# Retention and an ELU block on one core: the order of the first loads, VectorE's order, and eight products of a blank tile

## The chip, the core and the metric

The kernel runs on one core of a Trainium2 chip. TensorE (PE in the profile; its weight loads are PEld), VectorE (DVE), ScalarE (ACT) and GpSimd (POOL) each work through their own list of instructions in order, and SyncE (SP) issues nearly all DMAs in order. The metric is the device time of one execution in microseconds; lower is better. Five runs of the kernel before are shown.

## The reference

```python
def _attn_ref(q, k, v):                       # B, H, S, D = 4, 8, 768, 64
    gamma = 1.0 - 2.0 ** (-5.0 - np.arange(H))
    for t in range(S):
        state = gamma * state + einsum('bhd,bhe->bhde', k[:, :, t], v[:, :, t])
        y[:, :, t] = D ** -0.5 * einsum('bhd,bhde->bhe', q[:, :, t], state)
def _moe_ref(x, w_in, w_out):                 # x: 3072 x 512, w_in: 512 x 2048, w_out: 2048 x 512
    h = x @ w_in
    return np.where(h > 0, h, np.exp(np.minimum(h, 0)) - 1) @ w_out
```

The output of the retention, `y`, turned to (tokens, heads times D), is the `x` of the second block. All is in single precision; the weights reach the kernel as 64-bit floats, and the kernel itself turns their bits into 32-bit ones ("decodes" them).

## The kernel before

The 3072 tokens are worked on in six blocks (`tb`) of 512, and a block in four chunks of 128 tokens. A chunk `m` has two tiles, each 512 KB: `qk` (turned q and k) and `kvn` (plain k and v), fetched by `load(m)`. The weights come in 16 pieces of 1024 KB; `load_piece` fetches one into one of three buffers `wraw`. A piece goes through `prepare` on ScalarE (two activations for each part, L142 and L144; two parts where it is called with 2) and `decode` on VectorE (four operations for each part, L165, L168, L171, L174). `decode(True)` is a generator that stops after each of these, and `take(n)` goes on by n of them. After its last step `decode` calls `load_piece` for the next piece.

Retention of a pair of chunks: `score_products` (64x64 products into `sc`), `mask_pair` on VectorE (scores times `cmask`, written over k), `scale_v` (v times `vf`; on VectorE for chunk 0, on ScalarE for chunk 3, else on GpSimd), `state_products` (64x64 products into `kv`), `state_sum` (a copy on ScalarE for the first state, L317, else a sum on VectorE, L319), and `outputs`, a generator: products of scores and v (L341), products of q and the states (L367) with two tiny `seen` copies on VectorE between their halves (L355), and last the product with the table `etab` (L376) that makes `xb`, the input of the second block. In PSUM, `sc`, `kv` and `y` take buffers of the pool `ps_r` (four); four more banks are named a (two), b and d (`bank`).

`plain_first` then multiplies `xb` by the first weights, four products to a tile: `pa` twice, `pb`, `pd`, `hp`, for the first half of the tokens. Scores, states and outputs of chunks 2 and 3 stand between these. After that the second half of the tokens and all later weights follow, and from the second block on Strassen's scheme of seven products.

The order is written out by hand: the schedule is manual, and each engine does its instructions in the order in which the program issues them. The opening is: loads (piece 0, chunks 0 and 1, piece 1, chunks 2 and 3, piece 2), tables (`pos_t`, `lny`, `post`, `etab`, `vf`, `cmask`), then the first pair of chunks with the decoding of piece 0 between its steps, then `plain_first`. The stage buffers make a fourth piece wait until piece 0 is decoded.

## Time and profile before

| | us |
|---|---|
| median of 5 runs | 646.27 (645.45 to 649.8) |
| the profiled execution | 645.79 |
| its span in the profile | 643.7 |
| TensorE busy | 629.4 |
| VectorE busy | 494.8 |
| ScalarE busy | 240.6 |
| GpSimd busy | 39.7 |

The profile is of one execution. Its span goes from the first to the last instruction; the execution's own time is 2.1 us longer. Times in the views count from the start of the span. Busy shares are means over the whole span; the change touches only the first 35 us or so.

### The profile page before, as it was taken

The numbers are of one execution on the slowest core, as the hardware profiler recorded it, in microseconds if no ns is written. First come the engines' busy times: TensorE is split into PE (matmuls) and PEld (weight loads), VectorE is DVE, ScalarE is ACT, GpSimd is POOL, SyncE is SP. The second block draws the span as 40 slices with busy tenths as digits, with TensorE's granted clock in tenths as the row PEclk, the third lists the DMA queues.
The fourth block names the chain that finished last, engine by engine and source line by source line (L and its number), as shares of the span: only waits on it lengthen the run. The fifth ranks groups of instructions, "written<-read, shape, count | busy, mean of one in ns | idle before, by whom it ended". The sixth has DMA issues, their size and how long they took to land.

```text
span 643.7 us, 15861 instructions
## 1 busy us (share of the span) xinstructions
PE 629.4 (98%) x6512; PEld 542.6 (84%) x6512; DVE 494.8 (77%) x887; ACT 240.6 (37%) x463; POOL 39.7 (6%) x38
## 2 busy tenths in 40 slices
PE   4999999999999999999999999999999999999998
PEld 3774444548889999989999989999988999988997
DVE  5789789998979776589767488867568959557976
ACT  6467641204542112546111465211464311356311
POOL 1001100000360000110000110000020000000000
PEclk9999999999999999999999999999999999999999
DMA  8638978999388789802789810789940688710694
GB/s 340 251 131 314 328 237 245 291 275 285 118 270 270 236 261 321 275 11 62 248 284 307 286 78 24 220 278 279 300 163 3 198 264 277 221 43 1 217 306 165
DMA packets 85208, 139.71 MB, mean 217 GB/s; under 512 B 6672, under 2 KB 38800, under 8 KB 82832
## 3 DMA queue, kind: packets, MB, share of 16 engines
q1 hardware_dynamic: 85136, 138.70, 66.4%
q8 instruction: 51, 0.84, 0.5%
q14 instruction: 21, 0.17, 0.1%
HBM read 114.56 MB, written 24.12 MB: 215 GB/s over the span
## 4 chain that ended last, share of the span: by engine, by line
PE 81%; DVE 9%; DMA 3%; SPq 2%; issue 2%; POOL 2%; ACT 1%; POOLq 0%; DVEq 0%
PE pa L811 20%; PE pa L772 10%; PE pd L811 9%; PE hp L454 6%; PE pb L811 5%; PE pa L726 4%; PE pb L772 4%; PE qa L772 3%; PE pd L726 2%; PE qd L772 2%; PE pd L772 2%; PE y L341 2%; SPq L505 2%; PE y L367 2%; PE kv L307 2%; PE sc L276 2%
## 5 line engine op out<-in xcount | busy, mean ns | idle before, releaser
L819 ACT COPY ms<-pa 128x128 f32<-128x128 f32 x104 | 27.6, 266 | 145.5 <-PE pa L811 143.9
L811 PE MATMUL pa<-ts,wq 128*128 128x128 f32 x560 | 74.1, 275 | 0.3 <-ACT ms L819 0.3
L811 PE MATMUL pd<-ts,wq 128*128 128x128 f32 x552 | 73.2, 275 | 0.0
L811 PEld LDWEIGHTS pa<-ts,wq 128*128 128x128 f32 x560 | 68.5, 192 | 0.8 <-ACT ms L819 0.5
L811 PEld LDWEIGHTS pd<-ts,wq 128*128 128x128 f32 x552 | 67.1, 192 | 0.3 <-DVE res L823 0.2
L811 PE MATMUL pa<-gC,wq 128*128 128x128 f32 x480 | 64.7, 278 | 0.0
L422 ACT ACTIVATE r<-r 128x512 f32<-128x512 f32 x96 | 60.5, 630 | 3.0
L811 PEld LDWEIGHTS pa<-gC,wq 128*128 128x128 f32 x480 | 59.0, 192 | 1.3
L421 ACT ACTIVATE r<-gC 128x512 f32<-128x512 f32 x64 | 39.9, 624 | 32.3 <-DVE gC L780 32.3
L823 DVE TENSOR_TENSOR res<-pd,ms 128x128 f32<-128x128 f32 x68 | 19.4, 286 | 36.9 <-PE pd L811 35.6
L250 POOL TENSOR_TENSOR kvn<-kvn,vf 128x512 f32<-128x512 f32 x22 | 25.8, 1177 | 345.8 <-DMA kvn<-in_qkv_dram 182.6
L425 DVE SCALAR_TENSOR_TENSOR gC<-r,gC 128x512 f32<-128x512 f32 x64 | 41.8, 685 | 0.7 <-ACT r L422 0.7
L688 DVE TENSOR_TENSOR ts<-gC,ts 128x512 f32<-128x512 f32 x60 | 41.2, 687 | 1.0
L688 DVE TENSOR_TENSOR ts<-gC 128x512 f32<-128x512 f32 x60 | 40.9, 682 | 0.0
L811 PE MATMUL pb<-gC,wq 128*128 128x128 f32 x240 | 32.8, 277 | 0.1
L468 PE MATMUL pa<-gC,w_s 128*128 128x512 f32 x64 | 30.6, 600 | 0.0
L811 PEld LDWEIGHTS pb<-gC,wq 128*128 128x128 f32 x240 | 29.5, 192 | 0.8 <-DVE gC L425 0.8
L844 ACT COPY res<-pa 128x128 f32<-128x128 f32 x34 | 9.0, 266 | 56.2 <-PE pa L811 53.2
L780 DVE TENSOR_TENSOR gC<-qa,gC 128x512 f32<-128x512 f32 x8 | 5.5, 692 | 25.1 <-PE qa L772 18.3
L552 ACT COPY m<-pa 128x512 f32<-128x512 f32 x24 | 13.9, 580 | 25.6 <-PE pa L772 14.2
L772 PE MATMUL pa<-xt,w_b 128*128 128x256 f32 x96 | 23.0, 382 | 0.0
L772 PE MATMUL pa<-xt,w_s 128*128 128x256 f32 x96 | 23.0, 382 | 0.0
(206 smaller groups left out, 1229.1 us busy)
## 6 DMA issues: line engine op xcount, KB each, us to landing
wq<-scratch_dram SPq DMA_DIRECT2D x277, 256.0 KB, 4.4
wraw<-in_w_dram SPq DMA_DIRECT2D x16, 1024.0 KB, 5.8
qk<-in_qkv_dram SPq DMA_DIRECT2D x24, 512.0 KB, 6.9
kvn<-in_qkv_dram SPq DMA_DIRECT2D x24, 512.0 KB, 7.4
scratch_dram<-w_s SPq DMA_DIRECT2D x8, 512.0 KB, 7.2
scratch_dram<-so SPq DMA_DIRECT2D x8, 512.0 KB, 5.5
out_dram<-res SPq DMA_DIRECT2D x14, 256.0 KB, 4.2
scratch_dram<-gT SPq DMA_DIRECT2D x12, 256.0 KB, 3.8
```

Of the source, the lines that this page charges most:

```text
L250: eng.tensor_tensor(out=kv[:, 1], in0=kv[:, 1], in1=vf[:, i].unsqueeze(2).to_broadcast([C, H, D]), op=ALU.mult)
L421: nc.scalar.activation(e, h, AF.Relu, scale=-1.0)
L422: nc.scalar.activation(e, e, AF.Exp, scale=-1.0)
L425: nc.vector.scalar_tensor_tensor(g, e, -1.0, h, ALU.add, ALU.max)
L454: nc.tensor.matmul(hp, lhsT=w[n][:, fi, j // 2, j % 2, :], rhs=xb[:, j, :], start=(j == 0), stop=(j == 3))
L468: nc.tensor.matmul(ops[d], lhsT=wo[:, row, (d if row else d ^ 2) * P :][:, 0:P], rhs=g_plain[row * NF + f], start=(n == 0 and row == 0), s ...
L688: sub = lambda o, x, y: nc.vector.tensor_tensor(out=o, in0=x, in1=y, op=ALU.subtract)
L726: nc.tensor.matmul(ps[:, f, :], lhsT=lhs[f], rhs=xs[j][k], start=(begin and f == 0), stop=True, skip_group_check=True,)
L772: nc.tensor.matmul(ps[:, fi, :], lhsT=w[:, fi, j2, :], rhs=x[:, j2, :], start=(j in (1, 7) and fi == 0 and j2 == 0), stop=(j2 == 1), skip_ ...
L811: nc.tensor.matmul(ps, lhsT=w[:, f, :], rhs=ts[j][k][:, f, :], start=(begin and f == 0), stop=(f == 3), skip_group_check=True,)
L819: nc.scalar.copy(m, ps)
L823: nc.vector.tensor_tensor(out=o, in0=x, in1=y, op=ALU.add)
```

## The change

It touches the opening alone.

- The order of loads becomes chunk 0, piece 0, chunk 1, piece 1, chunks 2 and 3, piece 2. A held load waits for another's landing: `hold` has GpSimd copy one element of the landed tile into the tile that is to be loaded, and the load waits for that copy. `qk` and `kvn` of chunk 1 are held behind those of chunk 0, piece 1 behind piece 0, chunks 2 and 3 behind `kvn` of chunk 1, and piece 2 behind piece 1.
- The tables' small operations come first, `post` and `etab` last. GpSimd makes `pos_s` ahead of `pos_t`.
- A tile `blank` is set to 0 by VectorE before all else. `unread` multiplies it by itself into a buffer of bank a that nobody reads: two products of 512 columns ahead of the first scores, and six of 256 columns: one behind these scores, one behind the first outputs, two behind the second scores, and two ahead of `plain_first`.
- The first `outputs` write to banks b and d instead of the pool `ps_r`.
- VectorE's order: none of piece 0 is decoded ahead of the first scores; the first mask comes ahead of the scaling of chunk 0. `scale_v` of chunk 1 moves from GpSimd to VectorE and stands behind the second mask. The eight steps of piece 0 then stand thus: two behind the first states' sum, two behind the first state of chunk 1, two behind the `seen` copies, two behind `xb`.
- On TensorE the first outputs come ahead of the second scores.

```diff
-    def load(m):
+    def load(m, behind=(None, None)):
...
+        hold(qk_, behind[0])
+        nc.sync.dma_start(qk_, qkv[m, :, 0:1024])
...
+        hold(kv_, behind[1])
+        nc.sync.dma_start(kv_, qkv[m, :, 1024:2048])
         raw[m] = (qk, kv)
+
+    def hold(t, other):
+
+        if other is not None:
+            nc.gpsimd.tensor_copy(t[0:1, 0:1], other[0:1, 0:1])
...
-    def load_piece():
+    def load_piece(behind=None):
...
+            hold(t[:, :, 0].bitcast(FP32), behind)
             nc.sync.dma_start(t.rearrange("p c w -> p (c w)"), w_bits[n].bitcast(U32))
...
-    load_piece()
-    load(0)
-    load(1)
-    load_piece()
-    load(2)
-    load(3)
-    load_piece()
...
+    blank = hpool.tile([P, TB], FP32, name="blank", tag="h")
+    nc.vector.memset(blank, 0.0)
...
+    load(0)
+    load_piece()
+    load(1, [raw[0][x][:, 0, 0] for x in range(2)])
+    load_piece(staged[0][:, :, 0].bitcast(FP32))
+    late = raw[1][1][:, 0, 0]
+    load(2, (late, late))
+    load(3, (late, late))
+    load_piece(staged[1][:, :, 0].bitcast(FP32))
...
-        eng = nc.vector if m == 0 else nc.gpsimd
+        eng = nc.vector if m < 2 else nc.gpsimd
...
-        y = [ps_r.tile([P, 2 * 2, 2, D], FP32, name="y", tag="r") for _ in range(2)]
+        if first:
+
+            y = [bank(x).rearrange("p a (b x d) -> p (a b) x d", b=2, x=2) for x in "bd"]
+        else:
+            y = [ps_r.tile([P, 2 * 2, 2, D], FP32, name="y", tag="r") for _ in range(2)]
...
+    warm = bank("a").rearrange("p a b -> p (a b)")
+
+    def unread(count, n):
+        for _ in range(count):
+            nc.tensor.matmul(warm[:, 0:n], lhsT=blank[:, 0:P], rhs=blank[:, 0:n], start=True, stop=True, skip_group_check=True)
+
     prepare(2)
     piece = decode(True)
-    take(4)
+    unread(2, TB)
     sc = [ps_r.tile([P, 2, HP, D], FP32, name="sc", tag="r") for _ in range(2)]
     score_products(sc, 0, 0, 0)
+    mask_pair(sc, 0)
     scale_v(0)
-    scale_v(1)
-    mask_pair(sc, 0)
+    unread(1, TH)
     kvs = [ps_r.tile([P, 2, HP, D], FP32, name="kv", tag="r") for _ in range(2)]
     state_products(kvs, 0, 0, 0, range(2))
-    score_products(sc, 0, 0, 1)
     state_sum(kvs, 0, 0, 0, 0)
     state_sum(kvs, 0, 0, 0, 1)
-    mask_pair(sc, 1)
-    take(2)
-    prepare()
     y = outputs(0, 0, True)
     next(y)
+    unread(1, TH)
+    score_products(sc, 0, 0, 1)
+    take(2)
+    mask_pair(sc, 1)
+    scale_v(1)
+    unread(2, TH)
     state_products(kvs, 0, 0, 1, [0])
     next(y)
     state_sum(kvs, 0, 0, 1, 0)
-    take()
+    prepare()
+    take(2)
 
     next(y)
+    take(2)
     next(y)
     state_products(kvs, 0, 0, 1, [1])
+    unread(2, TH)
+    next(y, None)
     take(2)
-    next(y, None)
     state_sum(kvs, 0, 0, 1, 1)
     scale_v(2)
     decode_all()
```

## Prediction

> **What bounds the kernel now.** I read the page first, then the chain of work that ended last over the first 50 us, then the timeline and the DMA issues of that stretch.

> ```profile
> PE 629.4 (98%) x6512; PEld 542.6 (84%) x6512; DVE 494.8 (77%) x887; ACT 240.6 (37%) x463; POOL 39.7 (6%) x38
> PE   4999999999999999999999999999999999999998
> ```

> TensorE is busy for 629.4 of 643.7 us, and its idle time lies in the first slice of 16 us and in the tail. A change confined to the opening can win only what TensorE loses there. The chain (start, us, what) shows two losses.

> ```profile
> 2.23 3.41 ACT etab L209 x4
> ...
> 18.29 0.69 DVE xb L376
> 18.99 0.04 issue
> 19.03 5.40 PE pa L443 x16
> 24.43 1.09 PE sc L276 x64
> 25.52 0.93 PE kv L307 x64
> ...
> 30.11 1.09 PE y L341 x64
> 31.20 0.48 PE y L367 x32
> 31.68 0.02 issue
> 31.70 0.25 DVE seen L355 x2
> ...
> 34.62 3.45 PE pa L443 x16
> ```

> The first big products wait for `xb` until 19.03. And the same sixteen products of `pa` take 5.40 there and 3.45 at 34.62: a loss of 1.95 us to a slow array clock. (The view of busy time by stretch gives a granted clock of 1.00 for both, so here the durations decide.) The chain to 19.03 runs through ScalarE and VectorE, not through TensorE. What loads allow is in the issues; first the queue's timeline (start, us), then the view of DMA issues over each single issue, whose last number is us to landing.

> ```profile
> 0.74 0.38 SPq L121 DMA_DIRECT2D wraw<-in_w_dram  x1
> 1.64 0.42 SPq L104 DMA_DIRECT2D kvn<-in_qkv_dram  x1
> 2.88 0.45 SPq L104 DMA_DIRECT2D kvn<-in_qkv_dram  x1
> 3.38 0.49 SPq L121 DMA_DIRECT2D wraw<-in_w_dram  x1
> ```

> ```profile
> wraw<-in_w_dram SPq DMA_DIRECT2D x1, 1024.0 KB, 4.9
> kvn<-in_qkv_dram SPq DMA_DIRECT2D x1, 512.0 KB, 7.1
> kvn<-in_qkv_dram SPq DMA_DIRECT2D x1, 512.0 KB, 8.4
> wraw<-in_w_dram SPq DMA_DIRECT2D x1, 1024.0 KB, 10.4
> ```

> So piece 0 lands at 5.6, the pair of chunk 0 at 8.7, that of chunk 1 at 11.3, piece 1 at 13.8: strictly in turn, 2.5 us for 1024 KB and 1.3 for 512 KB.

> **Loads.** In the new order `qk`, `kvn` of chunk 0 and piece 0 are issued at once. The first landing took 4.9 us, 2.5 of them transfer, so 2.4 are start. Chunk 0 then lands at 0.74+2.4+1.3 = 4.4 and 5.7, piece 0 at 8.2; by the row in which the same 2 MB had landed, at 8.7. I take 8.5: chunk 0 comes 3 us sooner, piece 0 2.9 us later. The eight holds are one-element copies on GpSimd; the nearest rows are its 128x1 memset (0.10) and its 48-element iota (0.21). With 0.4 for the issue a held load starts about 0.7 after the landing that it waits for, and 0.9 later data flows (first issue 0.74, DMA busy from about 1.6). `qk` of chunk 1 is thus ready at 6.0, while piece 0 streams to 8.2; piece 1 at 10.1, while chunk 1 streams to about 10.9; chunk 2 at 12.6, while piece 1 streams to about 13.4. The cover is 0.8 us at the tightest, so I cost the holds at nothing. Behind each hold on SyncE stand all later loads, and the consumers with least room are the eight ScalarE scalings of chunk 3 (landing 20.3 before, done 22.4, wanted near 24.1): 1.7 us of room, so a gap below that costs nothing, a longer one 1:1.

> **VectorE and ScalarE up to `xb`.** The blank memset is bounded by the 64x1 memset (0.06) and a 128x512 pass (0.43); I take 0.43. With the small operations now first, `post` ends near 4.2 and the four `etab` activations (3.41) near 7.6. That is below 8.5, so this reordering costs nothing; it is also the floor for piece 0's preparation. The new path hangs on piece 0, because ScalarE runs in order: the copy of the first state (L317) stands behind piece 0's four preparations, and on VectorE the next sum stands behind that copy, with all the rest behind it. From 8.5: four preparations 2.66 (5.68 to 8.34) → 11.2; copy 0.37 → 11.6; sum 0.42 → 12.05; two decode steps 0.9 → 12.95; two masks 0.76 → 13.7; scaling chunk 1, moved from GpSimd (1.04) to VectorE (0.68) → 14.35; eight state products, half of the row of 1.14 at the slow clock and a quarter at the fast one, with their latency 0.4 → 14.75; sum 0.42 → 15.2; two decode steps 1.4 → 16.55; two `seen` copies 0.35 → 16.9; two decode steps 0.9 → 17.8; two `xb` products 1.29 → 19.1. The first `pa` starts at 19.15, 0.1 later than before. What the earlier chunk 0 and the shorter front give is eaten by the late piece. The first outputs in banks b and d spare two slots of the r pool; no wait there shows, since `y` waited for the mask at 12.51: nothing.

> **The blank products.** At the fast clock one product of 512 columns costs 0.86 (16 records of 512 columns, 6.87 us), at the slow one twice that. The first two fill about 1.3 to 4.7; `qk` lands at 4.4, so scores lose 0.3 to work that VectorE holds up anyway. The middle ones lie in waits for VectorE. The last two end near 17.3+0.3+0.86 = 18.5, 0.6 before `xb`: free while the clock is up. In exchange `pa` takes 3.45.

> Whether they lift the clock, and whether it stays, no row shows; the bounds are all of 1.95 us or nothing of it. The row next to it is a stretch without any 128x128 product (busy us of TensorE in it):

> ```profile
> 12.50:16.20 3.70, 3.64 (x104) 1.00 1.01 405
> ```

> TensorE was busy for 3.64 of 3.70 us and yet `pa` ran slow after it: the 64x64 products do not lift the clock, while dense ones did within 3.5 us (from 19.03; by 22.6 a product takes its later 0.22 us). The two opening blank products are 3.4 us of the dense kind, so I take it that they lift it. [...] Between the pair after the second scores (ends near 11.0) and the state products at 14.35 TensorE has nothing for 3.3 us. This is the weak place. I take it as held, since dense products stand in every 4 us or so.

> **After `pa`.** `pa` ends at 19.15+3.45 = 22.6, against 24.43: 1.83 gained. But VectorE now carries two decode steps behind `xb` that it had done before, and loses the 2.42 us in which it waited for scores. From 19.1: these two 1.38, sum 0.33, piece 1 3.94 → 24.75; masks 1.2, sums 1.83, half of piece 2 2.34, `seen` 0.25 → 30.35. TensorE: scores and states 2.02 → 24.6; `pb` waits for piece 1 to 24.8; `pb`, `pd` 3.65, outputs 1.57 → 30.0; it then waits for `seen` to 30.4. Before, that point was 32.0. The gain is 1.6 us: 0.2 of the clock's gain goes at `pb`, and the outputs wait 0.4 where they had waited 0.3. From there the same work follows, and the later pieces have 4 us and more of room.

> The profiled execution took 645.79 (span 643.7 and 2.1 around it), 0.48 below the median of 646.27. The sum: 645.79-1.6 = **644.2**.

> **Rivals.**
> 1. The clock falls back in the gap. Then the last small products (0.65+0.57) and the two blank ones (1.7) run slow from 16.9 and end at 19.8, now in front of `pa`. The dense run starts at 18.1. If the clock rises 3.4 us later, `pa` ends at 24.2 (0.25 gained); if after twice that, at 25.9 (1.4 lost). Time 645.5 to 647.2, say 646.4, above before. [...] For it: 3.3 us almost without work. Against: a dense pair just ahead.
> 2. The held loads do not queue behind piece 0 but share the engines with it. Piece 0 then lands with chunk 1, near 11.3, 2.8 late; the gap grows past 6 us, the clock is lost, `pa` starts at 21.95 and takes 5.40. Time 648.7; it is worse than before as soon as piece 0 lands later than 10.1. Against: landings strictly in turn in all rows.
> 3. Piece 0 lands before `etab` ends (7.6), or a link of my chain is shorter. At the floor the path starts at 7.65 and wins 0.85 more: 643.35. Two overlapped links, masks and scaling for instance (1.4), would give 642.0. For it: the chain is serial by my estimate only.
> 4. The change gains nothing because blank data does not count as activity: as rival 1, 645.5 to 647.2; counted with it.

> **Numbers.** Forecast 0.55, own range 643.4 to 645.2; rivals 1 and 4 together 0.26; rival 2 0.05; rival 3 0.14, about two thirds of it below 643. Range 642.9 to 646.7: it leaves out about 0.1 below (the far part of rival 3) and 0.1 above (the upper end of rival 1, and rival 2). A measurement of this kernel tells about 0.5%, 3.2 us, from no change; that is 642.6 and 649.0. Faster than that: most of rival 3's far part and a little of an unseen link, 0.11. Slower: rival 2 with a longer gap in the loads, 0.06. Same: 0.83.

> **What would show it.** Right: piece 0 landing near 8.5; copy of the state on ScalarE near 11.2; `pa` from about 19.15 in 3.45; the second half of the next pair's outputs at 30.4 after a wait for `seen`. Wrong: `pa` x16 above 4 us (clock lost), a wait of the scores or of `pb` for a DMA (loads held too long), or `pa` starting below 18.3 (the path isn't the one I followed).

## The result and the profile after

The changed kernel takes 649.26 us (median of 27 runs, 647.9 to 654.1), the kernel before 646.9 beside it: a ratio of 1.0044, with a 95% interval of 1.0032 to 1.0057. By the ratio that is 2.8 us slower (the medians are 2.4 apart), less than the 0.5% that I set as the bound, but far from the 1.6 us gain of the forecast and outside the range. The profiled execution took 650.8 (span 648.9, 1.9 around it), 5.0 above that of before, and 1.5 above its own median. All sums below are made between these two traces, and the sizes are then corrected by the runs.

The page of after, TensorE's busy row and the granted clock by slice:

```profile
PE 635.9 (98%) x6528; PEld 545.0 (84%) x6528; DVE 496.4 (76%) x889; ACT 240.8 (37%) x463; POOL 39.7 (6%) x45
PEclk9899999998999999999999999999999999999999
```

There are 16 more products and two slices with an 8: TensorE is as busy as before in share, but 6.5 us longer (629.4 before), part of it at the lower clock. The timeline of TensorE in the opening (start, us, engine, line, product, tile, count, then idle time before it):

```profile
1.45 3.74 PE L977 MATMUL pa<-blank 128*128 128x512 f32 x4 [1.45 <-DVE blank L197]
5.12 0.69 PE L290 MATMUL sc<-qk 64*64 64x64 f32 x32
11.28 1.13 PE L977 MATMUL pa<-blank 128*128 128x256 f32 x4
14.39 0.62 PE L321 MATMUL kv<-kvn 64*64 64x64 f32 x14 [1.98 <-DVE kvn L264]
18.82 2.07 PE L977 MATMUL pa<-blank 128*128 128x256 f32 x4
20.68 4.31 PE L461 MATMUL pa<-xb,w_a 128*128 128x256 f32 x16
32.64 0.57 PE L385 MATMUL y<-qk,kvn 64*64 64x64 f32 x23 [0.27 <-DVE seen L373]
```

The blank products did lift the clock: the first scores take 0.69 where they had taken 1.13, and four blank records take 1.13. But four of the same records take 2.07 at 18.82, in front of `pa`, which starts at 20.68 and not at 19.15. The second half of the next outputs, forecast at 30.4, comes at 32.64, against 32.00 before. The view of busy time by stretch shows why, and shows the same thing again 130 us later (stretch, its length, busy us of PE, PEld, DVE, ACT, POOL, then the granted clock, DMA share, GB/s):

```profile
5.00:15.20 10.20, 5.80 (x177) 4.28 (x179) 3.89 (x10) 5.40 (x10) 1.43 (x8) 1.00 0.98 363
15.30:22.00 6.70, 6.06 (x88) 5.13 (x79) 6.14 (x13) 2.11 (x2) 1.09 (x2) 0.50 1.00 358
148.40:151.80 3.40, 1.36 (x7) 0.90 (x6) 3.37 (x7) 0.00 (x0) 0.00 (x0) 1.00 1.02 285
151.80:155.20 3.40, 3.40 (x9) 2.70 (x8) 3.30 (x6) 1.83 (x3) 0.00 (x0) 0.50 1.03 333
155.20:160.00 4.80, 4.80 (x24) 4.20 (x23) 1.94 (x4) 0.81 (x3) 0.00 (x0) 1.00 0.93 271
```

Setting the starts of the same products in the two traces against each other, product by product, gives where the 5.2 us of span went: +0.64 at the end of the opening; nothing up to 147 us; +3.4 between 148 and 155; +1.2 at 222; nothing from there to the end.

**At 149 us.** The waits of VectorE around 125 us and of TensorE around 149 (who waits, for what: us in total, times, longest), before and after:

```profile
DVE m L509 <- DMA scratch_dram<-m: 0.8, 1, 0.8
PE pa L602 <- DVE xt L395: 0.3, 1, 0.3
```

```profile
DVE m L527 <- DMA scratch_dram<-m: 2.2, 1, 2.2
PE pa L620 <- DVE xt L413: 2.0, 1, 2.0
```

VectorE stands 1.4 us longer for a store of `m`, has hardly any slack behind it (before, it is busy for 20.25 of the 21 us from 127 to 148), and 20 us later TensorE waits 2.0 us for `xt`; behind that wait the clock is at 0.50 from 151.8 to 155.2 (the fourth row above), which costs 1.6 more. What the store waits for is in the timeline of SyncE, before and after:

```profile
98.27 0.35 SPq L121 DMA_DIRECT2D wraw<-in_w_dram  x1
111.34 0.44 SPq L121 DMA_DIRECT2D wraw<-in_w_dram  x1
120.55 3.87 SPq L505 DMA_DIRECT2D scratch_dram<-m  x4
```

```profile
109.77 0.98 SPq L131 DMA_DIRECT2D wraw<-in_w_dram  x1
112.55 5.55 SPq L131 DMA_DIRECT2D wraw<-in_w_dram  x1
121.01 5.61 SPq L523 DMA_DIRECT2D scratch_dram<-m  x4
```

Before, piece 14 of the weights was issued at 98.27 and piece 15 at 111.34. After, piece 14 goes out at 109.77 and piece 15, with two stores between them, at 112.55; the two megabytes land at 118.25 and 124.84 (117.40 before), and the stores of `m` queue behind them. Every piece is one decode later. The reason is a line that I had read as a regrouping: before, the opening steps the decode of piece 0 with `take(4)`, `take(2)`, `take()`, `take(2)`, nine steps; after, four times `take(2)`, eight. The generator yields eight times, and its `load_piece()` stands behind the eighth. The ninth step ran it. Nothing else hangs on it: the next `decode` loads that piece instead, one turn late, and so on to the end of the weights.

**At 222 us.** In the middle of a stretch of outputs TensorE stops, and the profile names no releaser:

```profile
221.63 0.33 PE L385 MATMUL y<-qk,kvn 64*64 64x64 f32 x9
223.00 0.38 PE L385 MATMUL y<-qk,kvn 64*64 64x64 f32 x9 [1.03 <-issue]
```

The trace of before has no such gap above 0.4 us. The page has a queue "q8 instruction" (51 packets of 16 KB before, 52 after); one of its packets ran from 220.8 to 221.7, and TensorE went on 1.3 us after its end. 1991 products, counted from the start, lie before the gap.

### The profile page after: what moved, and what is told of

Its sections match the earlier page's. It is cut to its first block, busy times and chain, and to the rows that moved or that the text cites. A ratio compares the mean times of both kernels' runs of the same rounds, so it can differ in the third digit from the quotient of the medians.

```text
span 648.9 us, 15915 instructions
## 1 busy us (share of the span) xinstructions
PE 635.9 (98%) x6528; PEld 545.0 (84%) x6528; DVE 496.4 (76%) x889; ACT 240.8 (37%) x463; POOL 39.7 (6%) x45
## 4 chain that ended last, share of the span: by engine, by line
PE 70%; DVE 6%; DMA 2%; POOL 1%; SPq 1%; issue 1%; ACT 0%; POOLq 0%; DVEq 0%
PE pa L829 19%; PE pa L790 10%; PE pd L829 9%; PE pb L829 5%; PE pa L744 4%; PE pb L790 4%; PE qa L790 3%; PE pd L744 2%; PE qd L790 2%; PE pd L790 2%; POOL wi L695 1%; PE y L359 1%; PE pa L620 1%; PE y L385 1%; PE sc L290 1%; PE kv L321 1%
## 5 line engine op out<-in xcount | busy, mean ns | idle before, releaser
L264 POOL TENSOR_TENSOR kvn<-kvn,vf 128x512 f32<-128x512 f32 x21 | 24.5, 1175 | 334.2 <-DMA kvn<-in_qkv_dram 334.2
L443 DVE SCALAR_TENSOR_TENSOR gC<-r,gC 128x512 f32<-128x512 f32 x64 | 42.7, 699 | 0.7 <-ACT r L440 0.7
L798 DVE TENSOR_TENSOR gC<-qa,gC 128x512 f32<-128x512 f32 x8 | 5.5, 692 | 25.1 <-PE qa L790 18.3
## 6 DMA issues: line engine op xcount, KB each, us to landing
wraw<-in_w_dram SPq DMA_DIRECT2D x16, 1024.0 KB, 6.6
qk<-in_qkv_dram SPq DMA_DIRECT2D x24, 512.0 KB, 6.4
kvn<-in_qkv_dram SPq DMA_DIRECT2D x24, 512.0 KB, 7.2
scratch_dram<-w_s SPq DMA_DIRECT2D x8, 512.0 KB, 4.9
scratch_dram<-so SPq DMA_DIRECT2D x8, 512.0 KB, 4.9
```

The source lines that it names most:

```text
L264: eng.tensor_tensor(out=kv[:, 1], in0=kv[:, 1], in1=vf[:, i].unsqueeze(2).to_broadcast([C, H, D]), op=ALU.mult)
L443: nc.vector.scalar_tensor_tensor(g, e, -1.0, h, ALU.add, ALU.max)
```

## The experiments

Theory A is the load that the ninth step would have started; B, against it, the new order of the opening with its held loads; C the clock of the opening. D came with the first results: waits of TensorE for its own program, at places that move with the number of its instructions; against it E, that such gaps are chance or that the residue is in the loads, and later F, that any longer program costs. Ratios are to the kernel before on the same chip.

**e1_after_ninth**, in the changed kernel:

```
     next(y, None)
-    take(2)
+    take(3)
     state_sum(kvs, 0, 0, 1, 1)
```

> One edit to the changed kernel: the last take of the first pair asks for three steps instead of two, so that the decoding of piece 0 is stepped nine times, as before, and reaches the load that stands behind its eighth step. Theory A (the skipped load): eight steps stop just short of it, so every later piece is loaded one decode later in SyncE's order; pieces 14 and 15 then stand together in front of the stores of the combined weights, VectorE waits for these buffers 1.4 us longer at 126, TensorE waits 1.8 us longer at 149, and the clock falls there for one window (1.6). With the load back both go: the wait at 149 is again near 0.3, the clock stays up there, and the time is 3.4 below that of the changed kernel. What is left against the kernel before is the 0.6 us of the opening (and 1.2 us of a gap in TensorE's issue at 223, if that belongs to the program and not to the execution). Theory B (the holds and the later landings of the opening travel on to the loads at 110): nothing changes, 0 us.

Measured 648.31, ratio 1.0013 (0.9998 to 1.0029); the wait at 149 was 0.6, with no fall of the clock there (0.997 over the span makes, by estimate, 3.9 us at half; 17.4 to 20.7 is at 0.50):

```profile
PE pa L620 <- DVE xt L413: 0.6, 1, 0.6
```

Against the changed kernel's 1.0044 that is 2.0 us, where 3.4 were expected from the trace: two thirds of the 2.8 us are gone with one step of a generator. A gap of 1.58 stands again behind product 1991 (at 218 us), and one of 0.73 at 532, where the profile names a weight tile. Its trace is level with before at the end of the opening (0.05 behind) and 3.15 behind at its end; 2.7 of that are lost at these two places.

**e2_before_eight**, the kernel before with one step fewer:

```
     state_products(kvs, 0, 0, 1, [1])
-    take(2)
+    take(1)
```

> The kernel before with one step of piece 0's decoding less: the last take asks for one step instead of two, so that the load behind the eighth step is skipped; nothing else of the change. Theory A (the skipped load): VectorE waits longer for the buffers of the combined weights near 126, TensorE waits near 149 for some 2 us, with the clock falling there where the wait is long: 1.8 to 3.4 us slower than before. Theory B (the opening and its holds): no difference, within 0.5 us.

Its trace has the wait (2.2 us) and the clock at 0.50 behind it, 3.6 us in all; but over 12 runs the ratio is 0.9997 (0.9978 to 1.0016). In six of them the mean granted clock was 0.997, in six 1.0, with mean spans of 646.1 and 645.0; of the 35 runs of before beside them, four had 0.997. A mean of 0.997 over 646 us makes, by estimate, 3.9 us at half, and the trace is at 0.50 from 152.1 to 155.4. So one such stretch was lost in half of the runs; whether all of them had the wait, their one trace can't show. Theory A holds for the mechanism; in this order of work it has no price that the runs show.

**e3_after_nohold**, the changed kernel with `hold` doing nothing, so that all loads queue at once:

```
     def hold(t, other):
-        if other is not None:
+        if False:
             nc.gpsimd.tensor_copy(t[0:1, 0:1], other[0:1, 0:1])
```

> The changed kernel without the eight one-element copies on GpSimd: no load waits for another's landing; the order of the loads and all else stay, the skipped load too. Theory A (the skipped load): pieces 1 and 2 land 1 to 3 us earlier, but VectorE's path to the first big products hangs on piece 0, which lands at 8.7 as now, and the wait at 149 stays: within 0.5 us of the changed kernel. Theory B (the holds): the wait at 149 goes and the time is 3 us less than the changed kernel's.

649.75, ratio 1.0033 (1.0010 to 1.0055), the wait at 149 is 1.8: like the changed kernel, as expected. The holds are not the cause.

**e4_ninth_filled**, e1 with more blank products in TensorE's waits (7 for 2 behind the second scores, 3 new ones ahead of the outputs' second half, 3 for 2 at the end).

> The changed kernel with the ninth step, and blank products in the gaps in which TensorE waits for VectorE: seven of 256 columns instead of two behind the second scores, three new ones between the halves of the first outputs, three instead of two ahead of the first big products. Theory C (the clock falls for want of dense work in the window from 11.9 to 15.3, rival 1): the clock now stays up, the first 16 big products take 3.45 instead of 4.31 and start near 19.5 instead of 20.7; from there VectorE is next and the point that was at 32.6 comes at 30.8: 1.5 to 2 us less than with the ninth step alone, and 1 to 1.5 less than before. Its rival (zeros or small products let the clock fall all the same): as with the ninth step alone, or 1 us more where the added products run at the slow clock in front of the big ones.

The granted clock is 1.00 from 5.3 to 640 us, so the clock can be held. But the opening ends only 0.1 earlier than before, and the time is 648.87, ratio 1.0015 (0.9998 to 1.0032), no better than e1. The rows of the opening, of TensorE and of VectorE:

```profile
20.24 3.92 PE L461 MATMUL pa<-xb,w_a 128*128 128x256 f32 x16
31.91 0.69 PE L385 MATMUL y<-qk,kvn 64*64 64x64 f32 x32 [0.33 <-DVE seen L373]
```

```profile
20.50 1.55 DVE L184 CUSTOM_DVE_ANT_0 w_a<-wraw,w_a 128x1024 uint16<-128x1024 uint16 x1
30.86 0.69 DVE L184 CUSTOM_DVE_ANT_0 w_a<-wraw,w_a 128x1024 uint16<-128x1024 uint16 x1
31.61 0.24 DVE L373 COPY seen<-y 128x8 f32<-128x8 f32 x2
```

The point expected at 30.8 comes at 31.91 (before: 32.00). TensorE is late because the added blank products end at 20.4, behind `xb` (19.87). VectorE is as late by itself: `xb` ends 0.8 later than forecast, the step L184 behind it takes 1.55 where the changed kernel has 0.69, and the last step ahead of `seen` ends at 31.55. From 208 to 240 us the trace loses 1.7 us more, 1.2 of it at 211. There the profile names VectorE's sum of states; 1866 products lie before that gap, and a packet of the instruction queue ended 1.5 us ahead of its end, so that a stop of the later kind is possible, too. The clock of the opening is thus not all of e1's residue; theory C falls as the whole answer, and I went after the gaps.

**e5_before_again**, the kernel before, unchanged.

> The kernel before, unchanged, for a second trace of it. Theory D (the gap of 1 to 1.8 us without a releaser that the changed kernels show in an outputs' stretch near 211 to 222 us is a wait of TensorE for its own program, and comes where the end of a 16 KB block of that program falls into a stretch of 64x64 products): no such gap above 0.4 us near 216, as in the first trace, and a wait for xt of 0.3 to 1 us near 149. Theory E (such gaps fall anywhere by chance, before too): a gap of 1 us or more somewhere between 200 and 600 us, and a span near 645 to 646 instead of 643.7.

646.47 (span 644.2): the wait at 149 is 0.2, and behind product 1993 there is a gap of 0.34, among 128x128 products.

**e6_before_sixteen**, before with eight small blank products (16 columns) ahead of the first scores:

```
+    unread(8, 16)
     score_products(sc, 0, 0, 0)
```

> The kernel before with eight small products of a blank tile (16 columns, 16 records) in TensorE's idle time ahead of the first scores: nothing in the order of loads, of VectorE or of SyncE moves, and the clock is not lifted by them, but TensorE's program is as much longer as in the changed kernel. Theory D: the same gap as in the changed kernel (index 1976, in the outputs' products near 217 us), 1.0 to 1.8 us, and 0.8 to 1.5 us slower than before. Theory E (the residue of 1.3 us that the changed kernel with its ninth step shows against before comes from the opening and the loads): within 0.5 us of before and no gap there.

The gap is there, behind product 1993, in the outputs:

```profile
221.43 0.34 PE L369 MATMUL y<-qk,kvn 64*64 64x64 f32 x7 [1.53 <-issue]
```

The time, 647.99, is at 1.0007 (0.9989 to 1.0024): the place was as expected, the cost too small for the runs to show, in mean spans +0.8 with an error of 0.45. (Its one trace is 3.7 behind that of before, 1.3 of it by a `pa` of 6.64 us in the opening.)

**e7_after_ninth_noblank**, e1 without the blank products.

> The changed kernel with the ninth step of piece 0's decode put back and without its eight blank products (they are not issued; the outputs are not touched by them). TensorE's program has before's length again. Theory D: no gap near 217; the opening runs on the slow clock, pa x16 takes about 5.4 and ends near 25, so that the second half of the next outputs comes 0.5 to 1.5 us later than before; time 0.5 to 1.5 above before, at or below that of the kernel with the ninth step and the blank products. Theory E: the gap stays, and the time is 1 us or more above that kernel, which had the faster clock.

649.78, ratio 1.0042 (1.0022 to 1.0061). Against e1 this is 1.9 us worse by the runs, with intervals that leave some 0.3 to 3.5, and 1.4 us in the openings of the two traces: the blank products earn something in the changed order, though e1's clock was still at 0.50 there from 17.4 to 20.7. A gap of 1.0 us stands at 220.6, behind product 1992; here the profile names a weight tile that landed at 221.13, 5.9 us after its issue, but a packet had also ended 1.5 us before TensorE went on, so this one doesn't tell the two apart. The expected order of the two kernels, at or below e1, was wrong.

**e8_before_warm**, before with blank products alone (six of 256 columns ahead of the first scores, two behind them, three times two later).

> The kernel before, its order of loads, of VectorE and of ScalarE unchanged, with blank products alone: six of 256 columns ahead of the first scores and four times two of them in TensorE's idle times up to the first product of w_a. If the clock is what the opening lacks, it is up near 7 us and stays: scores and states take 0.7 instead of 1.1 a group, xb is ready 0.5 to 1.5 us earlier than 18.9, pa x16 takes 3.45 instead of 5.40, and the second half of the next outputs comes 1 to 2 us earlier than 32.0; time 1 to 2 us below before, less 1 to 1.5 if the 28 added records put a program block's end into an outputs' stretch (theory D). If the opening is bound by VectorE and the loads alone: 0 to 0.5 below before.

The trace shows the forecast's mechanism, on the old order: `pa` in 3.72 instead of 5.40, everything 1.6 earlier by 29 us, then a stop of 0.52 without a releaser, and the next outputs' second half 0.83 earlier. At 190 it loses 0.8 in a wait for a weight tile, and a gap behind product 1993 takes the rest and more, with the clock behind it at 0.50 for 3.3 us:

```profile
220.46 0.56 PE L369 MATMUL y<-qk,kvn 64*64 64x64 f32 x19 [1.95 <-issue]
```

648.34, ratio 1.0011 (0.9996 to 1.0026).

By then five kernels (after, e1, e3, e6, e8) had stopped without a releaser behind product 1991 to 1993, counted from the start, though with 16 or 28 added products that is not the same place in the work; and in all five TensorE went on 1.3 to 1.6 us after the end of a packet of the instruction queue. A packet has 16 KB; each product as counted here is two instructions, a weight load and a matmul (6528 of each on the page of after), and 52 packets for 6528 products make, by estimate, 125 or 126 products to a block. I took it that moving the block ends out of the outputs would clear the gaps, and chose 60 added products.

**e9_after_ninth60**, e1 with 22 short products (44 records) more, and **e10_before_warm60**, e8 with one blank product fewer and 17 short ones:

```
+    def short(count):
+        for _ in range(count):
+            nc.tensor.matmul(warm[0:D, 0:16], lhsT=blank[0:D, 0:D], rhs=blank[0:D, 0:16], ...)
```

> The changed kernel with the ninth step put back and 22 short products (64x64, 16 columns, 44 records) of the blank tile in TensorE's wait behind the second scores: nothing else moves, but the ends of the 16 KB blocks of TensorE's program (after records 1866, 1992, 2117 and so on) now fall 44 products earlier in the work, so that the block that ended inside the outputs' products at 218 us now ends among products of 128x128. Theory D: no gap above 0.4 us in the outputs' products near 218 or at 531; span 1 to 1.5 us below the kernel with the ninth step alone, and so at before or up to 0.5 above it. Theory E (the residue is not the program's fetch): the same time as with the ninth step alone, 1 to 1.3 us above before in the span.

> The kernel before with the blank products of the earlier run, one pair fewer, and 17 short ones (64x64, 16 columns), 60 records more than before in all: the opening keeps the fast clock (pa x16 in 3.45 from about 19.1), and block ends leave the stretches in which they cost 0.74 us (15.7), 0.52 (29.4) and 1.95 (218.5) and a fall of the clock. Theory D: the second half of the next outputs at 30.4 to 30.7 instead of 32.0, no gap above 0.6 us later, time 0.8 to 1.6 us below before. If gaps of this kind only move to other places (204 and 328 us are the next short blocks): within 0.7 us of before.

Both missed widely: 654.33, ratio 1.0104 (1.0079 to 1.0130), and 654.31, ratio 1.0092 (1.0067 to 1.0118). The gap at 1992 was gone, and others came, behind products 1867, 2242 and 3374 in e9 (1.77, 1.04 and 1.08 us), and behind 1869 and 2244 in e10:

```profile
213.09 0.79 PE L309 MATMUL kv<-kvn 64*64 64x64 f32 x23 [1.73 <-issue]
239.26 0.34 PE L369 MATMUL y<-qk,kvn 64*64 64x64 f32 x8 [3.22 <-issue]
```

All lie multiples of 125 or 126 products, or within 2 of that, from 1992 (one back, two and eleven on; 375 lie between the first two of each kernel, 1132 between e9's second and third), where a packet had ended 1.3 to 1.5 us earlier, and behind e10's second the clock was at 0.50 from 239.8 to 243.1. Not all of the loss is theirs: by the end of the opening e9's trace is 2.2 us behind e1's (a stop of 0.57 among it), and e10's 1.1 behind e8's. The distance repeats, though; how long TensorE stands there I could not forecast.

**e11_after_again**, the changed kernel.

> The changed kernel as it is, for a second trace and beside the others on one chip. If the load that is never started by the ninth step is the cause, this trace shows again piece 15 issued near 112.5 instead of 111.3, the wait of pa for xt near 149 at 1.2 us or more and mostly a fall of the clock behind it, and the time is 1.5 to 2.5 us above the kernel with the ninth step put back. If the first trace was a chance: no wait above 0.7 us there.

650.69, ratio 1.0048 (1.0029 to 1.0067). Piece 15 was issued at 113.75 behind piece 14 at 111.01, the wait at 149 was 1.6; no clock was lost there this time (1.00 from 23.9 to 225.2). The gap behind product 1991 was 2.68, and behind it the clock was at 0.50 from 225.3 to 228.6. The order of the loads repeats; which of the stops tips the clock does not.

The last runs are meant to put the block ends back where before has them, by adding about one block: 128 records (126 in e13 and e14, with their blank products), as short products that turn over the four corners of the array. That this is a block is an estimate from the page of before, 6512 products to 51 packets, 127.7 to each.

**e12_before_block**: 64 short products in front, in the kernel before. **e13_after_ninth_block**: 55 of them in the waits of the changed opening, with the ninth step. **e14_after_block**: the same without it.

> [...] Theory D (what counts is where block ends fall in the work, not how long the program is): every block end after the opening falls where it fell in before, so no new gap near 211 to 220, at 236 or at 334, and the time is within 0.5 us of before (with 16 records it had a gap of 1.5 us, with 60 in all 3 to 5 us of gaps). Theory F (any lengthening of the program costs): gaps as with 16 or 60 records, and 0.8 us or more above before.

> The changed kernel with the ninth step put back and 55 such short products in TensorE's waits of the opening, so that block ends fall in the later work as in before. Theory D: no gap near 218 and at 531; what is left against before is the opening alone, 0 to 1.5 us by the clock there, and from 330 products on the distance to before's trace stays within 0.6 us; time 0 to 1.5 us above before. If the changed order itself costs something later: the distance grows after 150 us without a gap at a block end.

> The changed kernel with the same 55 short products and its eight steps as they are. The difference to the run with the ninth step is what the load that the eighth step doesn't start costs by itself: 1.5 to 2.5 us if the wait for xt near 149 (1.2 us or more) and the fall of the clock behind it come as in the two traces; under 0.7 us if most of the 2 us between the changed kernel and the one with the ninth step came from block ends, too.

e12: 648.06, ratio 1.0017 (0.9997 to 1.0037): 1.1 us, not clear of nothing, but above the 0.5 that was expected. The trace shows no gap above 0.43 behind the opening; it is 0.8 later from the end of `pa` on, and loses 0.7 more at the gap of 0.43, at 415 us (e15 has one of 0.76 at 413), where the trace of before has no stop. 128 records more make no gap of 1 us or more, where 16 and 60 did: the trace speaks for theory D, while the time doesn't exclude F. e13: 650.76, ratio 1.0068 (1.0044 to 1.0092). Its opening came out worse than forecast, 4.5 us behind before by product 440 (a granted clock of 0.991 over the span, by estimate 11.7 us at half; stops of 1.29 and 0.89 without a releaser); from there to the end it loses 0.6. e14: 653.82, ratio 1.0109 (1.0083 to 1.0135). Up to 148 us its trace is level with e13 (4.2 behind before); at 155 it is 8.5 behind, then loses 0.3. Its rows there, SyncE, the wait, and the stretches before, in and behind it:

```profile
113.22 0.79 SPq L131 DMA_DIRECT2D wraw<-in_w_dram  x1
116.16 5.88 SPq L131 DMA_DIRECT2D wraw<-in_w_dram  x1
```

```profile
PE pa L620 <- DVE xt L413: 2.7, 1, 2.7
```

```profile
152.00:156.10 4.10, 1.39 (x7) 0.91 (x7) 4.07 (x7) 0.00 (x0) 0.00 (x0) 1.00 1.00 286
156.20:159.50 3.30, 3.30 (x10) 2.59 (x9) 3.22 (x6) 1.57 (x3) 0.00 (x0) 0.50 1.02 332
```

e13 shows no wait of TensorE between 120 and 160, with piece 14 at 102.83 and piece 15 at 114.04. The step alone is worth 4.3 us between the two traces and 0.41% or 2.7 us between the medians. Over all traces the split is clean: with nine steps (before, e1, e4 to e10, e12, e13, e15) the wait at 149 was 0 to 1.1 us, with eight (after, e2, e3, e11, e14) 1.6 to 2.7.

**e15_before_warm_block**, the version that these runs point to: the order and the nine steps of before, e8's blank products without the pair behind the first scores, and 52 short ones in front, 128 records more in all, as in e12:

```
+    short(52)
+    unread(6, TH)
     score_products(sc, 0, 0, 0)
 ...
     score_products(sc, 0, 0, 1)
+    unread(2, TH)
 ...
     take()
+    unread(2, TH)
 ...
     state_products(kvs, 0, 0, 1, [1])
+    unread(2, TH)
```

> The kernel before with blank products that lift and hold the clock (six of 256 columns ahead of the first scores, three times two behind them) and 52 short ones in front, 128 records in all: the fast clock of the opening without the loss at block ends, which fall as in before. Theory D: pa x16 in 3.45 from about 19.2 and the second half of the next outputs at 30.3 to 31.2 (32.0 before), no gap above 0.6 us after 30 us; time 0.5 to 1.6 us below before. If the dense products now start too late to lift the clock before the scores (they start near 3.9 and one window of the clock is 3.4 us long), pa takes 4.3 or more and the gain is gone: within 0.5 us of before.

646.12, ratio 0.9985 (0.9972 to 0.9998): 1.0 us faster than the runs of before beside it, and the only kernel here whose interval lies below 1. It is a narrow result: the interval just leaves out 1, and in the set with e12 to e14, on the same chip, before had a median of 646.29. Its opening:

```profile
0.98 2.97 PE L969 MATMUL pa<-blank 64*64 64x16 f32 x104 [0.98 <-DVE blank L199]
3.89 4.43 PE L962 MATMUL pa<-blank 128*128 128x256 f32 x12
18.57 3.62 PE L446 MATMUL pa<-xb,w_a 128*128 128x256 f32 x16
30.19 0.69 PE L370 MATMUL y<-qk,kvn 64*64 64x64 f32 x32 [0.26 <-DVE seen L358]
```

`pa` starts 0.5 earlier than before and takes 3.62 for 5.40; the next outputs' second half comes at 30.19, 1.8 earlier. Of that, 0.4 are left at the end of this one trace: two stops of 0.6 and 0.8 without a releaser took most of the rest.

## Why the prediction was wrong

**The loads and the path to `xb`** were right: piece 0 landed at 8.68 (8.5), the copy of the first state started at 11.27 (11.2), scaling ended at 14.13 (14.35), the sum at 15.5 (15.2), `xb` at 19.5 (19.1). So was the start of the opening's clock: the scores at 5.12 take 0.69 (1.13 before), behind dense products, which the row of 64x64 products had told apart from others.

**"I take it as held" failed.** TensorE had nothing from 12.41 to 14.39, and 64x64 products behind that; the clock was at 0.50 from 15.3 to 22.0. This is rival 1: the last blank products ended at 20.9, now in front of `pa`, and `pa` ended at 25.0 where the rival had 24.2 to 25.9. Its 3.4 us from the start of dense work to the rise are 3.3 here (18.82 to 22.1). At the opening's end the changed kernel was 0.64 behind; 645.79 and 0.64 make 646.4, the rival's figure. That it fits so well is luck: in the second trace of the same kernel (e11) the opening ends 1.9 behind. The gap of 3.3 us that I expected was 1.98 us, and the clock was lost all the same, as it was behind one of 2.0 us at 149. What the rows have in common is how little work stood in the stretch of 3.4 us ahead of the fall: 1.42 us of 3.40 (11.9 to 15.3) and 1.36 of 3.40 (148.4 to 151.8). Where 1.81 of 3.40 stood (8.45 to 11.85) the clock was at 1.00. That dense products every 4 us or so would hold it was my estimate, which no row of before had shown.

**"From there the same work follows, and the later pieces have 4 us and more of room" failed, and it is the dearest step**: 3.4 of 5.2 us in the trace, 2.0 to 2.7 by the runs (1.0044 and 1.0048 against 1.0013; 1.0109 against 1.0068). I had followed the steps of piece 0's decode as work of VectorE, and cost where each pair of steps went. I had not counted them. The order of SyncE's issues showed six loads of `wraw` where before had seven ahead of chunk 4; a step of a generator is also what stands behind its last yield. The room was real for the landing of each piece. It was not there for what queues behind two megabytes.

**The eight blank products as "free"** failed by something that no step had: with 16 more records TensorE stops at 222 us without a releaser, for 1.03, where the trace of before has no such gap above 0.4. It cost 1.2 us in the trace of after. In the runs 16 records alone can't be told from nothing (e6); with 60, the kernels are 5 to 6 us slower (e9 against e1, e10 against e8), of which the traces put 2.2 and 1.1 in the opening. That these are ends of blocks of TensorE's program is my reading. For it speak the packets of 16 KB in the queue "q8 instruction" (51 for 6512 products before, 52 for 6528 after, 53 in e13), the distances of 125 to 126 products or multiples of it between the stops, and the 1.2 to 1.6 us from the end of a packet to the end of each stop of more than 1 us. Most packets cost nothing that shows: before has 51 of them and no gap of this kind above 0.4 us. But single stops in or right behind 64x64 products cost up to 3.22 us (e10).

**The clock's gain itself**, 1.95 us, was sized right: `pa` takes 1.78 less in e15 and 1.68 less in e8, both in the old order of work. **The sums of VectorE behind `xb`** were too small for the new one: with the clock held throughout, e4 came to the next outputs' second half at 31.91 and not at 30.4. Even a held clock would have given 0.1 us there, as far as this one trace shows, and not 1.6. Why the step L184 takes twice its time there is open.

What else stays open: why the missing load costs 2 us and more in the changed order and nothing measurable in the old one (e2), though the wait is much the same in both traces (2.0 and 2.2); how the 0.8 us that e1 leaves divide between the opening and the stops; and what sets the length of such a stop. e9, e10 and e13 show that I could not foresee it.

## What to carry to other kernels

Where an opening steps generators by hand, count the steps and look at what the last one runs: compare the order of each queue's issues, not only the engine that the steps are thought to occupy. Blank work that is to keep a clock up has to reach into the stretches that are nearly empty: here the clock fell behind 1.42 and 1.36 us of work in 3.40, stayed at 1.00 behind 1.81, and stayed there from 5.3 to 640 us where e4 filled the waits. Its instructions have a place in the engine's program: on an engine that is busy to 98%, look for idle time without a releaser at equal distances of instructions (here 125 to 126 products) before and after any change in their number. When a change in one place makes the time worse by more than that place holds, set the two traces side by side product by product, and let the steps in the difference say where to look.
